# Second MLP: output weights decoded in layer one and kept in DRAM, block sums on VectorE, accumulators read only when complete

## Chip, cores and metric

One core of a Trainium2 chip runs the whole program. The metric is the device time of one execution in microseconds (us); lower is better. Times before the change: 1127.17, 1128.53 and 1132.4 us, median 1128.53 us.

## What is computed

Causal attention with a decay, then two MLPs on its output, all in fp32:

```python
cum = np.cumsum(np.log(np.clip(f, 0.0001, 1.0)), axis=-1)
scores = scale * np.matmul(q, k.transpose(0, 1, 3, 2)) + cum[:, :, :, None] - cum[:, :, None, :]
attn = softmax(where(causal, -1e9, scores))          # q, k, v: 4 x 8 x 576 x 64
x = (attn @ v) -> (2304, 512)
h = x @ w_in;  x = (h - np.tanh(h)) @ w_out          # first MLP, 512 -> 2048 -> 512
h = x @ w_in2; out = np.maximum(h, 0.0) ** 2 @ w_out2  # second MLP, same sizes
```

## The kernel before

Every fp32 operand of a matmul is split into a high and a low part (hi, lo; ScalarE copies the rounded high part, VectorE or GpSimd subtracts it for the low one), and each product is three matmul passes: hi·hi, hi·lo, lo·hi. Attention and the first MLP fill the first 656 us or so; the change leaves their instructions in their order.

The second MLP is computed with seven block products in place of eight (a 2 x 2 block multiplication with sums of blocks ahead of it and additions behind it). It has two layers:

- **Layer one** (`layer1`, 24 units of 7 products: 3 groups of 768 tokens, for each 8 pairs `p` of hidden chunks). A product (`l1_product`, matmul L1072) is 6 matmuls of 384 columns. `after1` reads the PSUM banks: additions on VectorE L1084, a copy L1088 and relu L1098, L1102, L1107 on ScalarE. `store1` squares on GpSimd (L1113) and stores the result `g` to the DRAM scratch `gscr` (L1114).
- **Layer two** (`layer2`, 36 steps `n`: 9 token blocks `j` of 4 steps `q`, 7 products each). A step loads `g` from `gscr` in one DMA (`g_load`, L1154), forms four sums of 256 elements in `g_prep` (GpSimd L1162, L1163, L1165, VectorE L1164) and splits raw blocks and sums (ScalarE L1171, VectorE L1172) into a `gc` tile. A product (`l2_product`, matmul L1191) is 6 matmuls of 256 columns. The seven products share four PSUM banks, two to a bank for 1 and 6, 7 and 2, 5 and 4. After the block's last step `after2` reads them: VectorE L1204, ScalarE copy L1210, one addition on GpSimd L1211; then the output is stored.

The weights arrive in an encoded form: `load_w` fetches a pair, `decode_w` rebuilds the floats (ScalarE L178, L179, VectorE L185, L187), `combine` forms four sums on GpSimd (L229) and splits sums and raw blocks (ScalarE L248, lo parts L249 on GpSimd for the first piece, else VectorE). The output weights (phase 2) take the place of the input weights (phase 1) of the same pair, so they can be decoded only when the last group of tokens has used that pair: one per unit in units 16 to 23, the last ones in layer two.

The order is set in three ways. `cw.later(k, fn)` runs a follow-up after `k` more products; `feed.pace(goal)` starts at most one decode behind each product; and a list scheduler then orders each engine's queue by priority, with a bonus (`L2HOT`) for the start of layer two. SyncE (SP) issues all DMAs from one queue in order; every engine works its queue in order.

Layer two's products, and what their banks wait for:

```python
ORDER2 = (1, 6, 7, 5, 2, 4, 3)
if q == 3:
    cw.later(1, lambda: after2(j, k))       # behind every product
# after2, k == 6: copy bank 0, then
nc.gpsimd.tensor_tensor(t[:, 2], in0=t[:, 0], in1=t[:, 1], op=ALU.add)
# after2, k == 7: reads bank 1, into which product 2 is still to be written
add(t[:, 3], at(7), t[:, 2])
```

## Time and profile before

| | |
|---|---|
| median of 3 runs | 1128.53 us |
| profiled execution: time, span | 1124.71 us, 1123.0 us |
| granted TensorE clock, mean | 0.962 |
| TensorE busy | 1030.2 us (92%) |
| VectorE, ScalarE, GpSimd busy | 767.6, 597.5, 563.6 us |
| layer one of the second MLP | about 661 to 861 us |
| layer two | 861 to 1119 us |

The profile is one execution on the chip. Its page has a line of 40 slices for each engine, with the busy share in tenths; the timeline lists runs of like instructions of one engine with the idle time ahead of them and what ended it; the chain of waits follows the end back to what released each step. A busy TensorE isn't TensorE at its peak: its clock is granted at one of two levels (1.2 and 2.4 GHz), shown as a mean from 0.5 to 1.0. Layer one and layer two are the stages to read, each for itself.

### The profile page before, as it was taken

To read this page: it belongs to the slowest core of one execution; us is meant where nothing else is said; L and a number is where in the kernel's file an instruction comes from. 1 tells how busy PE (TensorE), PEld (TensorE's weight loads), DVE (VectorE), ACT (ScalarE), POOL (GpSimd) and SP (SyncE) were. 2 spreads that over 40 slices of the span, in tenths; PEclk is the share of its full clock that TensorE was granted. 3 is DMA by queue.
4 is the path that set the end of the run, shared out by engine and by line. 5 is a ranking of instruction groups with operands and counts; after the bars stand their busy time and mean duration, and the time that the engine had idled before them with its cause. 6 is when DMAs were issued, how large, how long until landed. Compare 5 with 4: busy or idle time off the path is not lost.

```text
span 1123.0 us, 20534 instructions
## 1 busy us (share of the span) xinstructions
PE 1030.2 (92%) x7246; PEld 981.5 (87%) x7246; DVE 767.6 (68%) x1579; ACT 597.5 (53%) x1256; POOL 563.6 (50%) x709
## 2 busy tenths in 40 slices
PE   7989999999999999999999989999984678888878
PEld 5778899999999999999987778999984678888878
DVE  5889835777777777777557763535688986666662
ACT  6879744666666667666446543434556442332220
POOL 4755523455545554564223444464577864444450
PEclk9999999999999999999999999999987788998899
DMA  8958433432433234321313252344555343332321
GB/s 221 261 171 248 145 96 79 123 84 65 130 86 106 79 93 115 91 69 47 86 59 110 76 160 94 113 144 143 186 171 165 122 132 94 101 107 94 95 94 38
DMA packets 152309, 131.76 MB, mean 117 GB/s; under 512 B 81328, under 2 KB 128752, under 8 KB 152208
## 3 DMA queue, kind: packets, MB, share of 16 engines
q1 hardware_dynamic: 152160, 130.43, 39.4%
q8 instruction: 57, 0.93, 0.3%
q14 instruction: 44, 0.36, 0.1%
q10 hardware_dynamic: 48, 0.03, 0.0%
HBM read 93.13 MB, written 32.58 MB: 112 GB/s over the span
## 4 chain that ended last, share of the span: by engine, by line
PE 54%; DVE 9%; DMA 8%; POOL 8%; issue 6%; ACT 3%; SPq 1%; DVEq 0%; POOLq 0%; ACTq 0%
PE y L915 13%; PE h L875 13%; PE r L1072 10%; DMA graw<-gscr 5%; PE o L1191 5%; DVE gc L1172 4%; PE pt L657 4%; PE pv L728 3%; POOL wsum L229 2%; PE s L619 2%; PE s L620 2%; DMA yr<-yscr 1%; POOL t L1211 1%; DMA wraw<-in_moe_w_in_dram 1%; DVE wfull L187 1%
## 5 line engine op out<-in xcount | busy, mean ns | idle before, releaser
L915 PE MATMUL y<-ghl,w 128*128 128x256 f32 (+1 forms) x1536 | 246.8, 303 | 3.0 <-DVE ghl L896 1.6
L915 PEld LDWEIGHTS y<-ghl,w 128*128 128x128 f32 x1536 | 210.1, 190 | 16.7 <-ACT ghl L892 2.8
L875 PE MATMUL h<-x,w 128*128 128x256 f32 x1344 | 200.0, 290 | 4.8 <-POOL w L201 3.7
L875 PEld LDWEIGHTS h<-x,w 128*128 128x128 f32 x1344 | 174.7, 191 | 9.7 <-POOL w L201 5.0
L1191 PE MATMUL o<-wq,gc 128*128 128x256 f32 x648 | 101.1, 302 | 47.3 <-DVE t L1204 33.2
L1191 PEld LDWEIGHTS o<-wq,gc 128*128 128x128 f32 x648 | 91.7, 208 | 49.7 <-DVE t L1204 35.0
L1191 PE MATMUL o<-ws,gc 128*128 128x256 f32 x864 | 128.1, 302 | 5.7 <-DVE gc L1172 3.3
L1191 PEld LDWEIGHTS o<-ws,gc 128*128 128x128 f32 x864 | 121.4, 212 | 6.4 <-DVE gc L1172 3.7
L450 POOL TENSOR_SCALAR Pb<-neg,ccol 128x384 f32<-128x384 f32 (+2 forms) x96 | 68.7, 715 | 91.7 <-PE pt L657 74.1
L1072 PE MATMUL r<-yt,ws 128*128 128x384 f32 x576 | 110.6, 340 | 2.9 <-DVE ys L925 2.9
L578 POOL TENSOR_SCALAR Pb<-Pb,st 128x384 f32<-128x384 f32 (+2 forms) x96 | 66.7, 695 | 82.2 <-DVE st L574 50.6
L1072 PEld LDWEIGHTS r<-yt,ws 128*128 128x128 f32 x576 | 102.8, 192 | 4.1 <-DVE ys L925 3.6
L1113 POOL TENSOR_TENSOR g<-g 128x768 f32<-128x768 f32 x48 | 75.2, 1582 | 61.6 <-ACT g L1102 59.4
L564 ACT ACTIVATE Pb<-Pb,st 128x384 f32<-128x384 f32 (+2 forms) x96 | 67.6, 704 | 68.0 <-DVE st L555 67.7
L1171 ACT ACTIVATE gc<-graw 128x512 fp32r<-128x512 f32 x72 | 33.7, 515 | 130.0 <-PE o L1191 85.2
L1072 PE MATMUL r<-yt,wq 128*128 128x384 f32 x432 | 88.7, 351 | 14.6 <-ACT g L1098 9.8
L1072 PEld LDWEIGHTS r<-yt,wq 128*128 128x128 f32 x432 | 80.0, 199 | 16.5 <-ACT g L1098 11.1
L555 DVE CUSTOM_DVE_ANT_0 Pb<-s,Pb 64x288 f32<-64x288 f32 (+2 forms) x160 | 73.8, 475 | 14.2 <-PE s L620 7.5
L1162 POOL TENSOR_TENSOR gs<-graw 128x256 f32<-128x256 f32 x36 | 33.6, 934 | 89.8 <-DMA graw<-gscr 86.7
L888 DVE TENSOR_TENSOR g<-h,g 128x512 f32<-128x512 f32 x72 | 49.5, 687 | 39.8 <-ACT g L885 38.4
L229 POOL TENSOR_TENSOR wsum<-wfull 128x256 f32<-128x256 f32 x32 | 31.0, 968 | 81.3 <-DVE wfull L187 80.7
L1172 DVE TENSOR_TENSOR gc<-graw,gc 128x512 fp32r<-128x512 f32 x72 | 63.8, 922 | 8.5 <-ACT gc L1171 8.5
(141 smaller groups left out, 2105.3 us busy)
## 6 DMA issues: line engine op xcount, KB each, us to landing
gscr<-g SPq DMA_DIRECT2D x48, 384.0 KB, 3.1
graw<-gscr SPq DMA_DIRECT2D x36, 512.0 KB, 3.6
wraw<-in_moe_w_in_dram SPq DMA_DIRECT2D x32, 512.0 KB, 4.7
wraw<-in_moe_w_out_dram SPq DMA_DIRECT2D x32, 512.0 KB, 5.2
neg<-cscr SPq DMA_DIRECT2D x32, 288.0 KB, 3.6
qk<-in_k_dram SPq DMA_DIRECT2D x48, 128.0 KB, 2.8
v<-in_v_dram SPq DMA_DIRECT2D x48, 128.0 KB, 2.7
K<-K SPq DMA_DIRECT2D x32, 144.0 KB, 2.4
```

The lines of the kernel that those rows point to most:

```text
L229: nc.gpsimd.tensor_tensor(o, in0=a, in1=b, op=op)
L450: nc.gpsimd.tensor_scalar(pb[:rows, o : o + w], t[:rows, :w], ccol[:rows, ti, b * H + h : b * H + h + 1], 1.0, op0=ALU.add, op1=ALU.mult)
L555: nc.vector.tensor_tensor_reduce(out=d, in0=t[:rows, src : src + m], in1=d, scale=-0.125, scalar=3.0e38 if j == 0 else stat(0, x)[:rows], ...
L564: nc.scalar.activation(d, d, AF.Exp, bias=stat(len(parts) - 1, x)[:rows], scale=-1.0, accum_out=stat(2, x)[:rows])
L578: nc.gpsimd.tensor_scalar(d, d, r, 1.0, op0=ALU.mult, op1=ALU.mult)
L875: nc.tensor.matmul(o, lhsT=win(fc, wh, dc), rhs=xpart(j, dc, xh), start=dc == 0 and wh + xh == 0, stop=dc == ND - 1 and wh == 1)
L888: nc.vector.tensor_tensor(g, t, g, op=ALU.subtract)
L915: nc.tensor.matmul(o, lhsT=wout(fc, wh, i * P, P), rhs=ghl[:, xh, fj * n : fj * n + n], start=s == 0 and fj == 0 and wh + xh == 0 and i % ...
L1072: nc.tensor.matmul(t, lhsT=wprod(1, p, k, wh)[:, dc * P : (dc + 1) * P], rhs=yt[i, k][:, xh, dc], start=k in FIRST and dc == 0 and wh + xh ...
L1113: nc.gpsimd.tensor_tensor(g, in0=g, in1=g, op=ALU.mult)
L1172: nc.vector.tensor_tensor(lo, in0=src, in1=hi.bitcast(F32), op=ALU.subtract)
L1191: nc.tensor.matmul(o, lhsT=gc[n][:, gh, GWHERE[k], e], rhs=wprod(2, 2 * q + e, k, wh), start=q == 0 and e == 0 and gh + wh == 0 and c0 == ...
```

## The change

The weights' two phases part ways. Phase 1 stays as it was, but for new tags, so that raw pieces of four pairs share tiles, and for lo parts, which are now all on VectorE. Phase 2 is decoded and summed during layer one from a raw tile of its own (one decode of phases 1 and 2 at a time), one pair per two units; the four sums and three raw quarters go to a DRAM scratch `wscr` as fp32 in three DMAs (0.92 MB). When the input weights of pair `p` are done with in the last group, `final_load` brings them back in one DMA and `final_split` splits them.

In layer two the four quarters of `g` come in four DMAs of 128 KB straight to their slots, three VectorE instructions form the sums, and hi and lo are one instruction of 1792 elements each. Steps 0 and 1 are loaded and summed in layer one. `gc` has three buffers (before four), the staging tile `graw` two; step n+4 is loaded right behind the split of step n+2. Banks are read only when both their products are done, and GpSimd's addition is on VectorE.

```diff
-L2HOT = 160
+L2HOT = 100
...
     def decode_w(phase, fc):
+        if phase:
+            if busy:
+                pending.append((phase, fc))
+                return
+            busy.append((phase, fc))
...
+        if phase == 2:
+            w = wscr[p]
+            nc.sync.dma_start(w[:, 0:4], sums.rearrange("p (k f) -> p k f", k=4))
+            f4 = full.rearrange("p (k f) -> p k f", k=4)
+            nc.sync.dma_start(w[:, 4:5], f4[:, 0:1])
+            nc.sync.dma_start(w[:, 5:7], f4[:, 2:4])
+            decoded()
+            return
...
-            (nc.gpsimd if x == 0 else nc.vector).tensor_tensor(lo, in0=src, in1=hi.bitcast(F32), op=ALU.subtract)
+            nc.vector.tensor_tensor(lo, in0=src, in1=hi.bitcast(F32), op=ALU.subtract)
...
+    def final_load(p):
+        t = box2["m2"].tile([P, 7, 256], F32, tag="xl", name=f"wst_{p}", bufs=2)
+        stagew[p] = t
+        nc.sync.dma_start(t, wscr[p])
+
+    def final_split(p):
+        t = stagew.pop(p)
+        split_all(2, p, split_plan(2, p, (t[:, 5:7], t[:, 4:5]), [t[:, 0:4]]), 1)
...
     def layer1():
...
-                elif i == 2:
-                    goal = 2 * NF
-            else:
-                goal = 2 * NF
+            if s >= PRE and (s - PRE) % 2 == 0 and (s - PRE) // 2 < NP2:
+                decode_w(2, (s - PRE) // 2)
+            if s >= PRE - 1 and (s - PRE + 1) % 2 == 0 and (s - PRE + 1) // 2 < NP2:
+                load_w(2, (s - PRE + 1) // 2)
+            if s == n - 3:
+                g_load(0)
+                g_load(1)
+            if s == n - 1:
+                g_sums(0)
+            if s == n:
+                g_sums(1)
...
-            if prev is not None and units1[prev][0] == 2:
-                feed.upload(NF + NP2 + units1[prev][1] + 1)
+            for p in range(NP2):
+                if s == last + FREED[p] - 1:
+                    final_load(p)
+                if s == last + FREED[p] + 1:
+                    final_split(p)
+
+    PRE = 5
+    FREED = (1, 2, 3, 3, 5, 6, 7, 7)
...
-    ORDER2 = (1, 6, 7, 5, 2, 4, 3)
+    ORDER2 = (1, 6, 7, 2, 5, 4, 3)
...
+        src = gscr[j // 3][:, j % 3, 4 * q : 4 * q + 4].rearrange("p (e i) (h t) -> p i h e t", i=2, h=2)
+        for slot, h, i in ((0, 1, 0), (5, 0, 0), (7, 1, 1), (6, 0, 1)):
+            nc.sync.dma_start(t[:, slot], src[:, i, h])
+
+    def g_sums(n):
+        t = graws[n]
+        x = t[:, 7]
+        both = bass.AP(tensor=x.tensor, offset=x.offset, ap=[x.ap[0], [0, 2], [1, 2 * P]])
+        nc.vector.tensor_tensor(t[:, 1], in0=t[:, 0], in1=t[:, 5], op=ALU.subtract)
+        nc.vector.tensor_tensor(t[:, 2:4].rearrange("p k e t -> p k (e t)"),
+                                in0=t[:, 0:2].rearrange("p k e t -> p k (e t)"), in1=both, op=ALU.add)
+        nc.vector.tensor_tensor(t[:, 4], in0=t[:, 6], in1=t[:, 3], op=ALU.subtract)
+
+    def g_split(n):
+        t = graws.pop(n)
+        c = box2["m3"].tile([P, 2, 7, 2, P], F32R, tag="gc", name=f"gc_{n}", bufs=3)
         gc[n] = c
...
+        nc.scalar.activation(c[:, 0], t[:, 1:8], AF.Copy)
+        nc.vector.tensor_tensor(c[:, 1], in0=t[:, 1:8], in1=c[:, 0].bitcast(F32), op=ALU.subtract)
...
-        if q == 3:
+        if q == 3 and k in (6, 2, 4, 3):
             cw.later(1, lambda: after2(j, k))
...
-            nc.gpsimd.tensor_tensor(t[:, 2], in0=t[:, 0], in1=t[:, 1], op=ALU.add)
-        elif k == 7:
+            add(t[:, 2], t[:, 0], t[:, 1])
+        elif k == 2:
             t = tmp2[j]
+            add(outs2[j][0][:, :256], at(2), t[:, 0])
             add(t[:, 3], at(7), t[:, 2])
...
         for n in range(NG):
...
             for x, k in enumerate(ORDER2):
                 if x == 1 and n + 2 < NG:
-                    g_prep(n + 2)
+                    g_sums(n + 2)
+                if x == 3 and n + 2 < NG:
+                    g_split(n + 2)
+                    if n + 4 < NG:
+                        g_load(n + 4)
                 cw.step(lambda: l2_product(n, k))
```

In the changed kernel the lines move: matmul of layer one L1138, of layer two L1270, load L1241, sums L1247, L1248, L1250, split L1256 (ScalarE) and L1257 (VectorE), `after2` L1283 and L1289, weight splits L294 and L295, stores to `wscr` L247, L249, L250, load from it L310.

**First excerpt: ScalarE, from the last unit of layer one into layer two.** `wraw`, `wfull`, `wsum`, `ws` and `wq` are weights (raw, decoded, summed, and split), with phase and pair in the name; `g1_23` is `g` of the last unit; `gc` and `graw` belong to steps of layer two. Before:

```order
L1102 ACTIVATE g1_23_10228<-g1_23_10228 128x768
L178 ACTIVATE wfull_2_6_10280<-wraw_2_6_10258 128x512
L179 ACTIVATE wfull_2_6_10280<-wraw_2_6_10258 128x512
L1107 ACTIVATE g0_23_10278<-g0_23_10278 128x3x128
L248 ACTIVATE ws_2_5_10272<-wsum_2_5_10267 128x512
L178 ACTIVATE wraw_2_6_10258<-wraw_2_6_10258 128x512
L179 ACTIVATE wraw_2_6_10258<-wraw_2_6_10258 128x512
L248 ACTIVATE wq_2_6_10324<-wfull_2_6_10280 128x256
L1171 ACTIVATE gc_0_10342<-graw_0_10337 128x512
```

Now:

```order
L294 ACTIVATE wq_2_1_2_10373<-wst_7_10262 128x512
L1171 ACTIVATE g1_23_10305<-g1_23_10305 128x768
L1176 ACTIVATE g0_23_10350<-g0_23_10350 128x3x128
L294 ACTIVATE ws_2_7_10376<-wst_7_10262 128x1024
L294 ACTIVATE wq_2_1_2_10373<-wst_7_10262 128x256
L1256 ACTIVATE gc_0_10393<-graw_0_10112 128x1792
L1256 ACTIVATE gc_1_10396<-graw_1_10117 128x1792
```

The decoding of pair 6 no longer stands around the end of layer one; two splits of pair 7 stand between the last relu and the first split of layer two.

**Second excerpt: VectorE in layer two, around the end of token block 2 (step 11).** `t2_2` and `os_2` belong to the evacuation of block 2, `o1_2` to `o3_2` are its banks. Before:

```order
L1172 TENSOR_TENSOR gc_14_11125<-gs_14_11124,gc_14_11125 128x1024
L1204 TENSOR_TENSOR t2_2_11067<-o1_2_10874,t2_2_11067 128x256
L1204 TENSOR_TENSOR os_2_1_11069<-o2_2_10875,t2_2_11067 128x256
L1204 TENSOR_TENSOR t2_2_11067<-o2_2_10875,t2_2_11067 128x256
L1204 TENSOR_TENSOR os_2_0_11068<-o3_2_10876,t2_2_11067 128x256
L1204 TENSOR_TENSOR os_2_0_11068<-o1_2_10874,t2_2_11067 128x256
L1164 TENSOR_TENSOR gs_16_11236<-graw_16_11228 128x256
L1204 TENSOR_TENSOR os_2_1_11069<-o2_2_10875,t2_2_11067 128x256
```

Now:

```order
L1248 TENSOR_TENSOR graw_13_10948<-graw_13_10948 128x512
L1257 TENSOR_TENSOR gc_12_10998<-graw_12_10895,gc_12_10998 128x1792
L1250 TENSOR_TENSOR graw_13_10948<-graw_13_10948 128x256
L1257 TENSOR_TENSOR gc_13_11056<-graw_13_10948,gc_13_11056 128x1792
L1283 TENSOR_TENSOR t2_2_11045<-t2_2_11045 128x256
L1283 TENSOR_TENSOR os_2_0_11046<-o1_2_10868,t2_2_11045 128x256
L1283 TENSOR_TENSOR t2_2_11045<-o1_2_10868,t2_2_11045 128x256
L1247 TENSOR_TENSOR graw_14_11001<-graw_14_11001 128x256
L1283 TENSOR_TENSOR os_2_1_11047<-o2_2_10869,t2_2_11045 128x256 x2
L1283 TENSOR_TENSOR t2_2_11045<-o2_2_10869,t2_2_11045 128x256
L1248 TENSOR_TENSOR graw_14_11001<-graw_14_11001 128x512
L1283 TENSOR_TENSOR os_2_0_11046<-o3_2_10870,t2_2_11045 128x256
```

Before, step 14 was split ahead of the evacuation; now its sums and its split stand behind it, and the last sum of step 13 behind the split of step 12.

**Third excerpt: SP's queue in layer one.** Stores of `g` have the unit in the name, stores to `wscr` the pair. Before, in units 19 to 21:

```order
L1114 DMA gscr_2_116<-g1_19_9872 384x1x256
L139 DMA wraw_2_3_9991<-in_moe2_w_out_dram 128x1024
L1114 DMA gscr_2_116<-g0_19_9950 384x1x256
L139 DMA wraw_2_4_10080<-in_moe2_w_out_dram 128x1024
L1114 DMA gscr_2_116<-g1_20_9961 384x1x256
```

Now, in units 12 to 14:

```order
L1183 DMA gscr_1_123<-g1_12_9456 384x1x256
L1183 DMA gscr_1_123<-g0_12_9519 384x1x256
L249 DMA wscr_6_93<-wfull_2_6_9796 128x256
L250 DMA wscr_6_93<-wfull_2_6_9796 128x512
L139 DMA wraw_2_7_9877<-in_moe2_w_out_dram 128x1024
L1183 DMA gscr_1_123<-g1_13_9530 384x1x256
L1183 DMA gscr_1_123<-g0_13_9593 384x1x256
L247 DMA wscr_6_93<-wsum_2_6_9865 128x1024
L139 DMA wraw_2_7_9877<-in_moe2_w_out_dram 128x1024
L1183 DMA gscr_1_123<-g1_14_9602 384x1x256
```

The loads of raw output weights moved seven units ahead, and stores to `wscr` stand between the stores of `g`.

## Rows read from the trace of the kernel before

**Rows 1.** The page, 40 slices of the span, busy tenths and granted clock:

```profile
PE   7989999999999999999999989999984678888878
PEclk9999999999999999999999999999987788998899
```

**Rows 2.** Windows: us, then busy us (count) of each engine, PEclk, DMA share, GB/s:

```profile
742.00:744.00 2.00, 2.00 (x14) 2.00 (x13) 1.07 (x3) 0.01 (x1) 1.92 (x2) 1.00 0.98 313
1000.00:1020.00 20.00, 15.77 (x116) 15.57 (x115) 13.56 (x18) 5.38 (x10) 10.30 (x11) 0.85 0.29 93
```

**Rows 3.** Timeline of TensorE, layer one: start, us, instructions, idle before and releaser:

```profile
796.16 2.24 PE L1072 MATMUL r<-yt,wq 128*128 128x384 f32 x12
...
803.44 2.24 PE L1072 MATMUL r<-yt,wq 128*128 128x384 f32 x12
...
813.05 2.35 PE L1072 MATMUL r<-yt,wq 128*128 128x384 f32 x12 [2.16 <-ACT g L1098]
...
824.03 4.21 PE L1072 MATMUL r<-yt,wq 128*128 128x384 f32 x12 [3.42 <-ACT g L1098]
...
845.98 3.47 PE L1072 MATMUL r<-yt,wq 128*128 128x384 f32 x12 [3.42 <-ACT g L1098]
```

**Rows 4.** Timeline of TensorE, layer two: its first, some middle and last instructions:

```profile
873.08 0.80 PE L1191 MATMUL o<-wq,gc 128*128 128x256 f32 x2 [11.86 <-ACT gc L1171]
...
989.50 1.29 PE L1191 MATMUL o<-wq,gc 128*128 128x256 f32 x7 [4.45 <-DVE t L1204]
...
1000.33 0.88 PE L1191 MATMUL o<-wq,gc 128*128 128x256 f32 x6
1001.05 0.88 PE L1191 MATMUL o<-ws,gc 128*128 128x256 f32 x6
...
1118.60 0.52 PE L1191 MATMUL o<-wq,gc 128*128 128x256 f32 x3
```

**Rows 5.** Waits from 840 us on: us in total, times, longest:

```profile
PE o L1191 <- DVE t L1204: 33.2, 9, 4.4
```

**Rows 6.** Chain of waits, end of a token block: start, us, what:

```profile
1013.47 1.67 POOL t L1211
1015.16 0.43 DVE t L1204
1015.64 4.16 PE o L1191 x18
```

**Rows 7.** Groups by form, 656 to 861 us: busy, mean ns, idle before:

```profile
L1113 POOL TENSOR_TENSOR g<-g 128x768 f32<-128x768 f32 x45 | 70.0, 1568 | 61.6 <-ACT g L1102 59.4 <-PE r L1072 1.8 <-POOL g L1113 0.3
L1084 DVE TENSOR_TENSOR g<-r,u 128x384 f32<-128x384 f32 x70 | 37.3, 550 | 43.4 <-DMA gscr<-g 34.1 <-PE r L1072 9.2
...
L187 DVE SCALAR_TENSOR_TENSOR wfull<-wraw 128x512 uint32<-128x512 uint32 x7 | 10.3, 1470 | 0.0
```

**Rows 8.** Line L1021 (loads of 128 KB in runs of 512 B), 700 to 760 us:

```profile
L1021 SPq DMA_DIRECT2D yr<-yscr x12: 378/528/627, 732.1 to 740.4; - x12
...
DMA to landing us min/median/max: 2.6/3.2/4.1
```

**Rows 9.** Groups by form, 861 to 1123 us:

```profile
L1171 ACT ACTIVATE gc<-gs 128x1024 fp32r<-128x1024 f32 x36 | 37.7, 1047 | 14.0 <-POOL gs L1165 8.0 <-DVE gs L1164 5.9
...
L1171 ACT ACTIVATE gc<-graw 128x512 fp32r<-128x512 f32 x36 | 22.7, 629 | 130.0 <-PE o L1191 85.2 <-issue 40.7 <-DMA gscr<-g 2.3
...
L1204 DVE TENSOR_TENSOR os<-o,t 128x256 f32<-128x256 f32 x36 | 14.9, 424 | 9.0 <-PE o L1191 7.3 <-issue 0.3
```

**Rows 10.** Timeline of VectorE and GpSimd, last steps of layer two:

```profile
1092.41 1.74 DVE L1172 TENSOR_TENSOR gc<-gs,gc 128x1024 fp32r<-128x1024 f32 x1
1093.03 1.70 POOL L1211 TENSOR_TENSOR t<-t 128x256 f32<-128x256 f32 x1
...
1098.51 1.03 DVE L1172 TENSOR_TENSOR gc<-graw,gc 128x512 fp32r<-128x512 f32 x2 [0.29 <-ACT gc L1171]
1099.76 1.23 DVE L1172 TENSOR_TENSOR gc<-gs,gc 128x1024 fp32r<-128x1024 f32 x1 [0.22 <-ACT gc L1171]
```

More of the change, by code (lines that the diff above doesn't have):

```diff
@@ L242, in combine @@
-        mixed = [(t1, 2 * x, 2, sums[:, 512 * x : 512 * x + 512].rearrange("p (c f) -> p c f", f=P)) for x in range(2)]
-        work = [(t2, k, n, src) for k, n, src in raw] + mixed
-        def part_split(x):
+        if phase == 2:
[6 more added lines that the diff above has]
+            return
@@ new lines, in combine, with raw_tile @@
+        v = full.rearrange("p (c f) -> p c f", c=ND)
+        s4 = sums.rearrange("p (k f) -> p k f", k=4)
+        work = split_plan(1, p, (v[:, :, 0:P], v[:, 2:4, P : 2 * P]), [s4[:, 0:2], s4[:, 2:4]])
+        split_all(1, p, work, 1)
+    wscr = [dram.tile([P, 7, 256], F32, name=f"wscr_{p}") for p in range(NP2)]
+    SUMTAG = (0, 2, 4, 6, 7, 9, 11, 13)
+    RAWTAG = ((1, 3, 5), (8, 10, 12))
+    rawt = {}
+    def raw_tile(phase, p, x):
+        key = (phase, p // 4, x)
+        if key not in rawt:
+            rawt[key] = wp.tile([P, 2, 4, 256], F32R, tag=f"w{RAWTAG[p // 4][x]}", name=f"wq_{phase}_{p // 4}_{x}", bufs=1)
+        return rawt[key]
@@ new lines, in raw_slots, with split_plan @@
+    def raw_slots(p):
+        r = p % 4
+        single = 3 * r if r == 1 else 3 * r + 2
+        double = 3 * r + 1 if r == 1 else 3 * r
+        return divmod(double, 4), divmod(single, 4)
+    def split_plan(phase, p, raws_, sums_):
+        t1 = wp.tile([P, 2, 4, 256], F32R, tag=f"w{SUMTAG[p]}", name=f"ws_{phase}_{p}", bufs=1)
+        (dx, d0), (sx, s0) = raw_slots(p)
+        td, ts = raw_tile(phase, p, dx), raw_tile(phase, p, sx)
+        wt[phase, p] = [(t1, k) for k in range(4)] + [(td, d0), (td, d0 + 1), (ts, s0)]
+        n = 4 // len(sums_)
+        work = [(t1, n * x, n, src) for x, src in enumerate(sums_)]
+        work += [(td, d0, 2, raws_[0]), (ts, s0, 1, raws_[1])]
+        return work
@@ L246, in part_split, with split_all, one @@
+    def split_all(phase, p, work, lag):
+        def one(x):
             t, k, n, src = work[x]
-            hi, lo = part(t, k, n, 0), part(t, k, n, 1)
+            f = src.shape[-1]
+            hi, lo = (t[:, hl, k : k + n].rearrange("p k f -> p (k f)").rearrange("p (c f) -> p c f", f=f)
+                      for hl in range(2))
             nc.scalar.activation(hi, src, AF.Copy)
-            (nc.gpsimd if x == 0 else nc.vector).tensor_tensor(lo, in0=src, in1=hi.bitcast(F32), op=ALU.subtract)
+            nc.vector.tensor_tensor(lo, in0=src, in1=hi.bitcast(F32), op=ALU.subtract)
@@ L974, in __init__ @@
         def __init__(self):
-            self.items = [(0, fc) for fc in range(NF)] + [(ph, p) for ph in (1, 2) for p in range(NP2)]
+            self.items = [(0, fc) for fc in range(NF)] + [(1, p) for p in range(NP2)]
             self.loaded = self.decoded = 0
@@ L1052, in stage_load @@
     def stage_load(i):
-        t = box2["m2"].tile([P, 5, 2, NU1], F32, tag="xl", name=f"yr_{i}", bufs=1)
-        r = dict(zip((3, 7, 1, 2, 5), (t[:, x] for x in range(5))))
+        r = {}
+        for ks in ((3, 7), (1, 2)):
+            t = box2["m2"].tile([P, 2, 2, NU1], F32, tag="xl", name=f"yr_{i}_{ks[0]}", bufs=2)
+            r.update(zip(ks, (t[:, 0], t[:, 1])))
+        r[5] = spare()[:, 3 * NU1 : 5 * NU1].rearrange("p (c n) -> p c n", c=2)
         for k in (6, 4):
@@ L1057, in stage_load, with spare @@
         y_load(i, r)
+    spares = []
+    def spare():
+        if not spares:
+            spares.append(wp.tile([P, 5 * NU1], F32, tag="w14", name="spare", bufs=1))
+        return spares[0]
     def blocks3(x):
@@ L1117, in layer1 @@
         n = len(units1)
+        last = n - NP2
         for s in range(n + 1):
@@ L1239, in layer2 @@
         with tc.high_priority(offset=L2HOT):
-            for n in range(2):
+            g_split(0)
+        with tc.high_priority(offset=L2HOT // 2):
+            g_split(1)
+            for n in (2, 3):
                 g_load(n)
-            for n in range(2):
-                g_prep(n)
-                for _ in range(4):
-                    cw.step()
         for n in range(NG):
-            if n + 2 < NG:
-                g_load(n + 2)
-            if n < 4:
-                feed.upto(NF + NP2 + min(NP2, 2 * n + 2))
             for x, k in enumerate(ORDER2):
                 if x == 1 and n + 2 < NG:
-                    g_prep(n + 2)
+                    g_sums(n + 2)
[3 more added lines that the diff above has]
+                        g_load(n + 4)
                 cw.step(lambda: l2_product(n, k))
-                feed.pace(NF + 2 * NP2)
     x_tile(0)
```

96 lines of the change are left out of this document (38 added, 58 removed).

## The prediction

> **What bounds the kernel now.** I read the page first. TensorE is busy nearly everywhere up to slice 29; from slice 30 (814 us) on its digits fall and the granted clock falls with them [rows 1]. The change touches only what lies there, the last 460 us, so I read the two layers of the second MLP each for itself; attention and the first MLP keep their order and their time.
>
> *Layer one* runs without a gap in its middle: the same group of matmuls starts at 796.16 and at 803.44, a unit of 7 products in 7.28 us, 1.04 us each. Then it starts at 813.05, 824.03 and 845.98, the last three units apart from the first: 10.98 us a unit [rows 3]. TensorE waits for ScalarE (relu L1098), whose queue there also holds the decoding of the output weights, one pair a unit, and the clock falls with the waits: 12 matmuls that took 2.24 us take 4.21 after a wait of 3.42, though only 2.35 after a wait of 2.16 [rows 3].
>
> *Layer two* starts 11.86 us after layer one's last matmul (873.08 less 11.86: 861.2) and ends at 1119.1 [rows 4]: 257.9 us. Six matmuls take 0.72 us (from 1000.33 to 1001.05), so 36 steps of 42 matmuls are 5.04 us each, 181.4 us in all; 76 us are waits and low clock. A middle stretch shows nothing full: TensorE 15.77 of 20 us, VectorE 13.56, GpSimd 10.30, the DMA engines 0.29, clock 0.85 [rows 2]. One wait repeats once per token block, 33.2 us over 9 [rows 5], 4.45 in one case [rows 4]. The chain shows what it is: GpSimd's addition takes 1.67 us, VectorE's reading of bank 1 0.43, and only then TensorE may write product 2 into that bank [rows 6].
>
> **The change part by part.**
>
> *The tail of layer one.* At 7.28 us a unit the group of 813.05 would start at 810.72, and that of 845.98 at 832.56: 13.4 us earlier. From 845.98 nine products are left, 9.36 us, so the layer would end at 841.9 and not at 861.2: **-19.3**. The first excerpt shows why it should: the decoding has left ScalarE's queue there.
>
> *What layer one gets for it.* Eight decodes, now in two units (14.56 us) each. VectorE has ten additions of 0.55 in them [rows 7], and a decode's four instructions and four lo parts, which I bound by 1.47 each from the dearest of them [rows 7], 11.8: 17.3 at worst, over the 14.56; at 0.66 each, as I work out below for 512 elements unhindered, 10.8. GpSimd has four squares of 1.57 [rows 7] and four sums, at most 1.67 each like its other addition of 256 elements [rows 6]: 13.0. ScalarE, at 0.63 for 512 elements [rows 9], has eight more, 5.0. It fits, tightly in units 7 and 15, where the tokens of the next group are split too. Price: nothing, up to one lost period of the tail per decode, 8 x 3.70 = 30. The tail had a decode in every unit, the change in every second, so I take the near end: **+4**, one such loss.
>
> *DMA in layer one.* Per two units 1.57 MB of `g`, 1.05 of raw weights, 0.92 to `wscr` and later back. In the fullest stretch 0.63 MB took 2 us at a share of 0.98 [rows 2], 3.1 us per MB: 11.1 of 14.56 us. Hidden, with little to spare. On SP each is an issue of about half a microsecond [rows 8], nine in 14.56 us; but a store to `wscr` waits for GpSimd's sums with the next store of `g` and the next raw load queued behind it (third excerpt).
>
> *The start of layer two.* Behind the last product stand an addition (0.55), two short activations (at most 0.63 each), a split of 1024 on ScalarE (1.05) [rows 7, 9], and then step 0's split. For 1792 elements I extend the rows: ScalarE 0.629 for 512 and 1.047 for 1024 [rows 9], 0.82 per 1000 elements, so 1.67; VectorE 1.03 for 512 and 256 together and 1.23 for 1024 [rows 10], 1.12 per 1000 and 0.09 fixed, so 2.09, and 0.66 for 512. Sum **6.6** before steady work, in place of 11.86 and stalls.
>
> *VectorE's speed.* That took the durations with GpSimd idle. Beside GpSimd's addition at 1093.03 the split of 1024 took 1.74 us, with GpSimd idle 1.23 [rows 10]; the changed kernel has no GpSimd work in layer two. Per step VectorE then has sums 0.42 + 0.66 + 0.42, a split of 2.09 and a quarter of seven additions of 0.42 [rows 9], 4.3 of 5.04 us. At 1.74/1.23 of that it would be 6.1, above TensorE. The Trainium skill ("GPSIMD Engine Reference", Specifications) says that GpSimd shares its SBUF interface with VectorE, with contention for instructions with two SBUF inputs; the rows agree, and by it the 4.3 stands.
>
> *The bank wait* goes: nothing is read before its bank is complete (ORDER2, `after2`). What is late next is the data. Two staging tiles pass load, sums and split, and VectorE takes things in its order (second excerpt). I walk one token block from the end of the split of step 10, in us: load of 12, three more issues of 0.53 and 3.2 to landing [rows 8], 4.8; last sum 0.42; ScalarE 1.67; VectorE 2.09; last sum of 13 0.42; 1.67; 2.09; evacuation 7 x 0.42 = 2.9; sums of 14 1.5; 1.67; 2.09, the split of 14. That is 21.3, and with nine hand-overs of 0.05 (from 1015.59 to 1015.64 in [rows 6]) 21.8, where TensorE needs 20.16. So the loop paces, by 1.6 us a block: 8 x 1.6 = **13**. Bounds: landing at 2.6 and 4.1 [rows 8] moves it by -0.6 and +0.9 a block, and more where a second landing comes on the path; every instruction 5% off moves it by 0.8. So 0 to about 27.
>
> *Clock.* The first wait, of 6.6, costs 2.0 like the one of 3.42; eight waits of 1.6, like the one of 2.16, 0.1 each: **3**.
>
> *At nothing:* tags, the order of additions, and the evacuation at the very end, which is as long as before.
>
> **Sum.** Layer two 6.6 + 181.4 + 13 + 3 = 204.0 against 257.9: -53.9. Span 1123.0 - 19.3 + 4 - 53.9 = 1053.8; with the 1.7 that lie around the span (1124.71) 1055.5. The median of the runs shown is 3.8 above the profiled execution; I add half, as three runs spread over 5: **1057**.
>
> **A rule against the change.** Twelve loads of 128 KB were issued within 8.3 us and each landed 2.6 to 4.1 us after its issue [rows 8]; one after the other they would need 38, so they overlap. The Trainium skill ("DMA: Bandwidth & Descriptors", Bandwidth and Anatomy of one DMA) wants DMAs of 1 MiB and more, and gives about 2.0 us plus bytes/436e3 for one: as an estimate 2.3 us for 128 KB, 9.2 for four in turn where the loop has 4.8, 35 us more over 8 blocks, 1092. By that rule the third rival would be the likeliest; the rows show loads side by side and leave it the chance it has.
>
> **The rivals.**
> - *TensorE paces layer two.* If loads land at 2.6 and sums hide beside other work, the loop is below 20.16 and the 13 go: 1057 - 13 - 1 = 1043. For it: the second and third landing need not be on the path. Against: VectorE's in-order queue. Chance 0.18.
> - *Layer one stalls again.* A square, a sum or a relu behind a decode, or SP held by a `wscr` store: from 4 to 8 lost periods of 3.70 less the 4 counted, 11 to 26 more: 1068 to 1083. For it: VectorE's worst case is over its time. Against: units 796 to 810 run unbroken with squares and stores. Chance 0.13.
> - *The loop is longer.* Four loads at once land later (4.1 or more, both landings on the path), 2 to 4 us more a block: 1073 to 1089; at the far end they are served in turn, 4 x 2.6 = 10.4 in place of 4.8, 45 us more: 1102. For it: 512 B runs in fours. Against: DMA share 0.29 now. Chance 0.12.
> - *VectorE stays slow* without GpSimd: 6.1 a step, 36 x 1.06 = 38 more than TensorE's pace, 1057 - 13 + 38 = 1082, and more with the loop. The rows of the last steps speak against it: 0.03.
> - *Slower than before:* the 14.7 MB through `wscr` make layer one bound by transfers. To reach 1128 plus half a percent it must lose 77 us in eight pairs of units, 9.6 us each: 3.54 MB in 24 us, below 150 GB/s. Rows show 313 GB/s at share 0.98 [rows 2]. 0.02.
> - *The change doesn't do what it says* (decoding still in the tail): the excerpts show it gone. Nil.
>
> **How the numbers follow.** The forecast has 0.52, from 1048 to 1066. The range 1039 to 1080 takes in nearly all of the first rival and over half of layer one's and some of the third: 0.52 + 0.16 + 0.09 + 0.05 = 0.82. A measurement here tells about 0.5% (6 us) from no change; every case but the one slower is 40 us or more below 1128.5, and some of that chance I leave to cases not thought of: faster 0.95, same 0.02, slower 0.03.
>
> **What would show it.** Layer one ends near 846 with units of 7.28 us up to the end. The first steady matmul of layer two comes 6 to 7 us later. TensorE's waits for VectorE's reading of banks are gone; in their place a wait of about 1.6 us at the third step of each block, for the split. VectorE's split of 1792 takes about 2.1 us, pieces of `graw` land in about 3.2. GpSimd is idle in layer two. Units of 11 us in layer one, splits of 3 us, or landings above 5 would make it wrong.

## The result and the profile after

The changed kernel takes 1075.65 us (median of 4 runs, 1074.40 to 1076.56) against 1127.85 us (4 runs) before: ratio 0.953, 95% interval 0.950 to 0.957. The profiled execution took 1074.4 us with a span of 1072.7. That is faster, as forecast, and inside the range, but 18.7 us above the 1057. Two errors of opposite sign lie behind this: layer one ended 27.1 us later than forecast (873.0, not 845.9), and layer two took 8.3 us less (195.7, not 204.0; before 257.9). That the time is inside the range is in part luck: layer one's miss by itself makes 1084, outside it.

The page, against [rows 1]: from slice 34 on, in layer two, TensorE's digits are 9 up to the last and GpSimd is idle. What is left stands in slices 27 to 33, from 697 to 885 us, where GpSimd works too.

```profile
PE   7989999999999999999999999988788869999997
...
POOL 4763622465455654556411333655655440000000
```

The windows say the same, against [rows 2]: 100 us of layer one with TensorE busy for 82.62, 160 us of layer two with 159.78.

```profile
750.00:850.00 100.00, 82.62 (x442) 77.21 (x442) 62.69 (x94) 44.19 (x77) 55.05 (x42) 0.98 0.65 213
```

```profile
890.00:1050.00 160.00, 159.78 (x1332) 159.58 (x1331) 122.53 (x171) 55.77 (x39) 0.00 (x0) 1.00 0.43 126
```

TensorE's timeline, against [rows 3, 4]. The waits of [rows 3] have moved forward: three of the longer ones now lie at 726, 756 and 774. Groups of 12 that take 2.24 us at full clock take 3.25 and 3.51. Layer one ends at 881.43 less 8.39, 873.04. Layer two has one wait of note behind its start, at 1058.70, and ends at 1068.8.

```profile
726.36 3.25 PE L1138 MATMUL r<-yt,wq 128*128 128x384 f32 x12 [2.40 <-ACT g L1167]
...
755.73 1.31 PE L1138 MATMUL r<-yt,ws 128*128 128x384 f32 x6 [2.27 <-DVE g L1150]
...
774.49 3.51 PE L1138 MATMUL r<-yt,wq 128*128 128x384 f32 x12 [2.86 <-ACT g L1167]
...
881.43 0.80 PE L1270 MATMUL o<-wq,gc 128*128 128x256 f32 x2 [8.39 <-ACT gc L1256]
...
1058.70 0.74 PE L1270 MATMUL o<-wq,gc 128*128 128x256 f32 x4 [1.89 <-DVE gc L1257]
...
1067.91 0.88 PE L1270 MATMUL o<-wq,gc 128*128 128x256 f32 x6
```

The waits from 661 to 873 us name the cause's neighbours. TensorE waits for VectorE's additions and for ScalarE's relu (24.1 us in all), VectorE's decode (L200) waits 21.8 us for ScalarE's, and ScalarE itself waits 28.4 us, in eight waits, for raw weights to land:

```profile
DVE wfull L200 <- ACT wfull L194: 21.8, 5, 6.3
ACT wfull L193 <- DMA wraw<-in_moe_w_out_dram: 21.4, 5, 5.5
...
PE r L1138 <- DVE g L1150: 15.1, 14, 2.4
...
PE r L1138 <- ACT g L1167: 9.0, 5, 2.9
ACT wraw L193 <- DMA wraw<-in_moe_w_out_dram: 7.0, 3, 4.3
```

The chain of waits shows how the two hang together. VectorE ends a decode (L202), GpSimd forms its sums (L244), SP may then store them (L247), and only behind that store can it issue the next raw load (L139). The load lands 5.51 us later. The next decode already stands in ScalarE's queue, ahead of the relu (L1167); the relu waits with it, and TensorE for the relu:

```profile
716.62 0.80 POOL wsum L244 x2
...
718.79 0.33 SPq L247
...
719.69 5.51 DMA wraw<-in_moe_w_out_dram
...
725.27 0.06 ACT wfull L193
...
725.83 0.48 ACT g L1167
...
726.36 3.26 PE r L1138 x12
```

Layer two, VectorE behind the end of a token block: seven additions of the evacuation with the sums of the next step between them, then a pair of splits.

```profile
966.13 0.42 DVE L1283 TENSOR_TENSOR t<-t 128x256 f32<-128x256 f32 x1
966.47 0.42 DVE L1283 TENSOR_TENSOR os<-o,t 128x256 f32<-128x256 f32 x1
...
969.39 0.42 DVE L1250 TENSOR_TENSOR graw<-graw 128x256 f32<-128x256 f32 x1
...
971.71 3.96 DVE L1257 TENSOR_TENSOR gc<-graw,gc 128x1792 fp32r<-128x1792 f32 x2 [0.37 <-ACT gc L1256]
```

The groups from 873 us on give the durations that the forecast extended, 1.70 us on ScalarE (forecast 1.67) and 2.02 on VectorE (2.09):

```profile
L1257 DVE TENSOR_TENSOR gc<-graw,gc 128x1792 fp32r<-128x1792 f32 x36 | 72.1, 2024 | 21.6 <-ACT gc L1256 21.4
L1256 ACT ACTIVATE gc<-graw 128x1792 fp32r<-128x1792 f32 x36 | 60.5, 1699 | 117.4 <-DVE graw L1250 107.1 <-PE o L1270 7.5 <-DVE wq L295 2.8
```

and the loads of `g` (line L1241) their landing, against [rows 8]:

```profile
DMA to landing us min/median/max: 2.1/2.6/4.1
```

### The profile page after: what moved, and what is told of

It reads as the page before. It is cut to its first block, busy times and chain, and to the rows that moved or that the text cites. A ratio compares the mean times of both kernels' runs of the same rounds, so it can differ in the third digit from the quotient of the medians.

```text
span 1072.7 us, 20563 instructions
## 1 busy us (share of the span) xinstructions
PE 1014.9 (95%) x7246; PEld 963.7 (90%) x7246; DVE 755.3 (70%) x1596; ACT 587.0 (55%) x1176; POOL 435.5 (41%) x576
## 5 line engine op out<-in xcount | busy, mean ns | idle before, releaser
L1256 ACT ACTIVATE gc<-graw 128x1792 fp32r<-128x1792 f32 x36 | 60.5, 1699 | 117.4 <-DVE graw L1250 107.1
L1138 PE MATMUL r<-yt,ws 128*128 128x384 f32 x576 | 111.0, 340 | 12.9 <-DVE g L1150 12.8
L1138 PEld LDWEIGHTS r<-yt,ws 128*128 128x128 f32 x576 | 100.9, 190 | 18.2 <-DVE g L1150 13.6
L1270 PE MATMUL o<-ws,gc 128*128 128x256 f32 x864 | 117.0, 285 | 0.0
L1270 PEld LDWEIGHTS o<-ws,gc 128*128 128x128 f32 x864 | 110.4, 194 | 0.0
L1182 POOL TENSOR_TENSOR g<-g 128x768 f32<-128x768 f32 x48 | 80.3, 1683 | 54.2 <-ACT g L1171 36.3
L1270 PE MATMUL o<-wq,gc 128*128 128x256 f32 x648 | 92.3, 287 | 10.5 <-ACT gc L1256 8.4
L1138 PE MATMUL r<-yt,wq 128*128 128x384 f32 x432 | 86.6, 343 | 11.9 <-ACT g L1167 9.0
L1270 PEld LDWEIGHTS o<-wq,gc 128*128 128x128 f32 x648 | 84.7, 195 | 11.5 <-ACT gc L1256 8.7
L1138 PEld LDWEIGHTS r<-yt,wq 128*128 128x128 f32 x432 | 76.8, 192 | 15.2 <-ACT g L1167 10.6
L1257 DVE TENSOR_TENSOR gc<-graw,gc 128x1792 fp32r<-128x1792 f32 x36 | 72.1, 2024 | 21.6 <-ACT gc L1256 21.4
L720 DVE TENSOR_TENSOR PT<-pt,PT 128x384 fp32r<-128x384 f32 (+2 forms) x96 | 55.1, 574 | 10.3 <-ACT PT L719 5.6
L951 DVE TENSOR_TENSOR ghl<-g,ghl 128x512 fp32r<-128x512 f32 x72 | 53.8, 747 | 10.2 <-ACT ghl L947 9.9
```

The lines of the kernel that those rows point to most:

```text
L720: cw.later(LAG['trlo'], lambda: nc.vector.tensor_tensor(dst[1], src, dst[0].bitcast(F32), op=ALU.subtract))
L1138: nc.tensor.matmul(t, lhsT=wprod(1, p, k, wh)[:, dc * P : (dc + 1) * P], rhs=yt[i, k][:, xh, dc], start=k in FIRST and dc == 0 and wh + xh ...
L1182: nc.gpsimd.tensor_tensor(g, in0=g, in1=g, op=ALU.mult)
L1256: nc.scalar.activation(c[:, 0], t[:, 1:8], AF.Copy)
L1257: nc.vector.tensor_tensor(c[:, 1], in0=t[:, 1:8], in1=c[:, 0].bitcast(F32), op=ALU.subtract)
L1270: nc.tensor.matmul(o, lhsT=gc[n][:, gh, GWHERE[k], e], rhs=wprod(2, 2 * q + e, k, wh), start=q == 0 and e == 0 and gh + wh == 0 and c0 == ...
```

## The experiments

In the profiles of these kernels E is the end of layer one, the first steady matmul of layer two less the wait ahead of it. In the changed kernel it is 873.0. Ratios and their 95% intervals are to the kernel before, run again beside each group of experiments; its median was 1130.6 us beside 1 to 4, 1131.8 beside 5 to 8, 1134.4 beside 9 to 11 and 1131.0 beside 12, against 1127.85 beside the change. So a time in us compares with the change's to some 3 to 7 us only, and the traces (one of each kernel) say where it went.

**1. No decoding in layer one**: what the new work costs there in all.

```diff
-        nc.sync.dma_start(t, wscr[p])
+        nc.sync.dma_start(t.rearrange("p k f -> p (k f)"), gscr[0].rearrange("p b c n -> p (b c n)")[:, 0:1792])
...
-            if s >= PRE and (s - PRE) % 2 == 0 and (s - PRE) // 2 < NP2:
-                decode_w(2, (s - PRE) // 2)
-            if s >= PRE - 1 and (s - PRE + 1) % 2 == 0 and (s - PRE + 1) // 2 < NP2:
-                load_w(2, (s - PRE + 1) // 2)
```

> The changed kernel without the decoding of the output weights: no raw loads, no decode, no sums and no stores to the scratch; the final load takes as many bytes from the scratch of g instead, so layer two multiplies other numbers, at the same instructions. Theory (what layer one lost, from 842 us where it would have ended to 873, is the decoding): layer one ends at 842 to 848 us, TensorE waits less than 6 us in it, time 1047 us (1043 to 1053). Rival A (the loss has other causes: lo parts now on VectorE, the token splits in units 7 and 15): layer one still ends after 860, time 1063 or more.

Measured: 1040.8 us (ratio 0.921, 0.915 to 0.927), E 838.1, and layer two as long as with the decoding (195.6 us). That is the theory, and a little below its numbers; TensorE waits 1.0 us in the layer. So the decoding costs layer one 35 us, and the tail's gain was there in full: 838.1, where the forecast had 841.9 ahead of this price.

**2. The next raw load ahead of the sums' store.** It is issued when the last read of the raw tile has been queued.

```diff
+                if phase == 2 and fc + 1 < NP2:
+                    load_w(2, fc + 1)
...
-            if s >= PRE - 1 and (s - PRE + 1) % 2 == 0 and (s - PRE + 1) // 2 < NP2:
-                load_w(2, (s - PRE + 1) // 2)
+            if s == PRE - 1:
+                load_w(2, 0)
```

> The changed kernel with one edit: the load of the next raw weights is given right behind the last read of the raw tile, so that in the DMA queue it stands ahead of the store of the four sums, not behind it. Theory (a loop through in-order queues: the raw load waits in SP's queue for GpSimd's sums, ScalarE waits in order for its landing, VectorE and GpSimd behind ScalarE): ScalarE's waits for raw weights, 28 us in the changed kernel, fall below 15, and half of the loss comes back: 1058 to 1066 us. Rival B (VectorE and GpSimd have too much to do in these units, whatever the order): within 3 us of 1075.6.

Measured: 1070.7 us (0.946, 0.941 to 0.952), E 869.5. Neither theory's number came. The waits for raw weights are down from 28.4 to 2.8 us, but others took their place. `wfull` and the sums share a ring of two tiles, and the next decode now waits until the sums' store has left the tile:

```profile
ACT wfull L193 <- DMA wscr<-wsum: 20.8, 6, 5.6
```

**3. The first ScalarE instruction of a decode kept in program order**, so that the scheduler can't put it ahead of the relu.

```diff
-            nc.scalar.activation(lo_, words[:, :, 0], AF.Copy, scale=0.936 * 2.0 ** -29)
+            ins = nc.scalar.activation(lo_, words[:, :, 0], AF.Copy, scale=0.936 * 2.0 ** -29)
+            if phase == 2 and x == 0:
+                tc.keep_in_program_order(ins)
```

> The changed kernel with one edit: the first ScalarE instruction of each decode of output weights is kept in program order on its engine, so that it stands one to two units later than where the scheduler had pulled it. Theory (ScalarE stands in order ahead of its data): its waits for raw weights fall below 8 us, layer one ends before 860, time 1052 to 1064 us. Rival B (too much work whatever the order): within 3 us of 1075.6.

Measured: 1073.4 us (0.950, 0.946 to 0.954), E 866.8. By the time this is rival B, and no difference to the change that is clear of noise. But it was half an experiment: the decode's second instruction (L196 here) was still put ahead, and waits in the first one's place.

```profile
ACT wfull L196 <- DMA wraw<-in_moe_w_out_dram: 15.9, 5, 5.3
```

The start of layer two grew from 8.39 to 12.10 us as well.

**4. Experiments 2 and 3 together.**

```diff
...
+            if phase == 2 and x == 0:
+                tc.keep_in_program_order(ins)
...
+                if phase == 2 and fc + 1 < NP2:
+                    load_w(2, fc + 1)
...
```

> Both edits, the raw load ahead and the decode kept in program order. Theory: waits for raw weights nearly gone, layer one ends at 846 to 854 us, time 1048 to 1058 us. Rival B (too much work whatever the order): 1070 us or more.

Measured: 1072.3 us (0.949, 0.945 to 0.952), E 867.6: by the time rival B again. The ring's wait stays, and one wait of TensorE is new: the decode of the last input weights stands behind the first one of output weights, now held at its place, waits for the ring there, and its split (L298) comes late.

```profile
720.73 1.01 PE L1142 MATMUL r<-yt,ws 128*128 128x384 f32 x2 [6.29 <-ACT ws L298]
```

**5. The early load, and sums in tiles of their own** (two of 512 elements, from another ring).

```diff
-        sums = wide(f"wsum_{phase}_{p}", F32)
...
+            halves = [m1.tile([P, 512], F32, tag="g", name=f"wsum_{p}_{x}", bufs=3) for x in range(2)]
...
-            nc.sync.dma_start(w[:, 0:4], sums.rearrange("p (k f) -> p k f", k=4))
+            for x in range(2):
+                nc.sync.dma_start(w[:, 2 * x : 2 * x + 2], halves[x].rearrange("p (k f) -> p k f", k=2))
```

> The raw load ahead (as before in this study) and one edit more: the four sums of output weights get tiles of their own, two of 512 elements that layer one leaves unused, so that the two decode buffers hold decoded weights alone; the store of the sums becomes two DMAs. Theory C (after the raw load was put ahead, ScalarE waited 20.8 us for the store of the sums to land, because the next decode needs that buffer: the loop closes over the two buffers): those waits fall below 6 us, layer one ends before 860, time 1055 to 1064 us. Rival B (VectorE and GpSimd have too much to do in these units): within 4 us of 1070.7.

Measured: 1066.7 us (0.944, 0.940 to 0.947), E 864.9: 4 less than experiment 2, at the edge of rival B's range and short of the theory's. The ring's waits are gone. With nothing else to hold them, the decodes were put earlier in ScalarE's queue again, and wait for the raw data once more:

```profile
ACT wfull L193 <- DMA wraw<-in_moe_w_out_dram: 17.0, 6, 5.5
```

**6. The transfers alone**: loads and stores as in the change, from a tile of zeros, and no instruction of the decoding.

```diff
+        if phase == 2:
+            wraw.pop((phase, fc))
...
+            for x in range(2):
+                nc.sync.dma_start(w[:, 2 * x : 2 * x + 2], z)
+            nc.sync.dma_start(w[:, 4:5], z[:, 0:1])
+            nc.sync.dma_start(w[:, 5:7], z)
+            decoded()
+            return
```

> The changed kernel with the loads of raw output weights and the stores to the scratch (from a tile of zeros, in four DMAs), but without decode and sums; layer two multiplies by zeros. Rival D (the transfers themselves, 14.7 MB more, slow the stores of g and with them layer one): time 1055 or more, layer one ends after 852. Theory B or C (the work on the engines and its order, not the transfers): within 5 us of the run without any decoding, 1036 to 1046 us.

Measured: 1046.5 us (0.925, 0.921 to 0.929), E 841.7, 3.6 over experiment 1. The transfers and SP's issues for them are not the cost, as long as no store among them waits for a result.

**7. The decoding without GpSimd's sums.**

```diff
-        sums = wide(f"wsum_{phase}_{p}", F32)
+        sums = wide(f"wsum_{phase}_{p}", F32) if phase == 1 else full
...
-        for o, a, b, op in ops:
+        for o, a, b, op in (ops if phase == 1 else ()):
...
-            nc.sync.dma_start(w[:, 0:4], sums.rearrange("p (k f) -> p k f", k=4))
+            nc.sync.dma_start(w[:, 0:4], full.rearrange("p (k f) -> p k f", k=4))
```

> The changed kernel with the output weights decoded, but without the four sums on GpSimd; the decoded weights are stored in their place, so layer two's numbers are others. Theory E (GpSimd's four sums per decode are what costs: squares stand behind them in order, and VectorE's instructions run slow beside them): most of the 35 us comes back, 1042 to 1056 us. Rival F (the cost lies with ScalarE and VectorE, whose decode instructions stand ahead of relu and additions): 1062 or more.

Measured: 1064.0 us (0.941, 0.936 to 0.946), E 862.8: rival F. Without the sums ScalarE still waits 27.3 us for raw weights (28.4 in the changed kernel).

So the sums are 10.2 of the 35 us, and the decode on ScalarE and VectorE, with its waits for raw weights, 21.1 (862.8 less 841.7). The two runs lie 5.1 us apart and the trace is of the longer one, so the sums' part may be larger.

**8. The kernel before with the new evacuation alone**: the order of the products, banks read when complete, GpSimd's addition on VectorE.

```diff
-    ORDER2 = (1, 6, 7, 5, 2, 4, 3)
+    ORDER2 = (1, 6, 7, 2, 5, 4, 3)
...
-        if q == 3:
+        if q == 3 and k in (6, 2, 4, 3):
...
-            nc.gpsimd.tensor_tensor(t[:, 2], in0=t[:, 0], in1=t[:, 1], op=ALU.add)
+            add(t[:, 2], t[:, 0], t[:, 1])
...
```

> The kernel before with one part of the change alone: the order of products in a token block and the reading of banks only when complete, with GpSimd's addition on VectorE. Theory (the bank wait, 33.2 us over 9 blocks, set layer two's end; data would have come in time): 30 to 42 us faster, 1086 to 1099 us. Rival (GpSimd's sums and the loads set the pace by themselves, so that TensorE waits for data in place of banks): less than 15 us faster, 1113 or more.

Measured: 1100.6 us (0.973, 0.970 to 0.976); layer two takes 227.7 us, 30 less than before. That is the theory's gain at its near end (31 us less than the kernel before beside it), but its reason holds in part only. The bank waits of [rows 5] are gone; the data doesn't come in time, and TensorE now waits for splits 20 times in 36 steps, 21.7 us in all. From 974 to 1043 us every step has such a wait, and they lie 6.3 us apart in the mean where 42 matmuls need 5.04:

```profile
992.65 1.45 PE L1191 MATMUL o<-ws,gc 128*128 128x256 f32 x10 [0.91 <-DVE gc L1172]
...
998.72 1.45 PE L1191 MATMUL o<-ws,gc 128*128 128x256 f32 x10 [0.78 <-DVE gc L1172]
```

Behind them, in its waits, is the way of the data over GpSimd's sums. The bank waits had hidden it. (These are idle times of GpSimd and ScalarE, not of TensorE.)

```profile
POOL gs L1162 <- DMA graw<-gscr: 78.2, 27, 4.1
ACT gc L1171 <- POOL gs L1165: 65.1, 30, 4.8
```

**9. Both orders at once**: experiment 5 with both first ScalarE instructions of a decode (from pair 1 on) and the first of each final split kept in program order.

```diff
+            if phase == 2 and fc and x == 0:
+                tc.keep_in_program_order(ins[0])
...
+                tc.keep_in_program_order(ins[1])
...
+            if phase == 2 and x == 0:
+                tc.keep_in_program_order(ins)
```

> Raw load ahead and sums in tiles of their own, and now both ScalarE instructions that open a decode (from the second pair on) and the first of each final split are kept in program order; in the two earlier runs of that kind only the first of the two was, and the second was still pulled ahead of its data. Theory C (in-order queues: whatever stands on ScalarE ahead of its data holds relu, VectorE and GpSimd behind it): ScalarE's waits for raw weights and for stores to the scratch fall below 4 us, layer one ends at 846 to 856 us, time 1050 to 1060 us, faster than the changed kernel by 15 or more. Rival B (VectorE, slowed by GpSimd beside it, has too much to do): within 4 us of 1066.7.

Measured: 1064.0 us (0.940, 0.935 to 0.944): by the time rival B. But E is 857.1, 7.8 less than in experiment 5, and the waits for raw weights are down to 2.3 us. The final splits, held too, came late, and layer two's start gave back 4.6 us of it (13.21 for 8.57):

```profile
870.29 0.79 PE L1283 MATMUL o<-wq,gc 128*128 128x256 f32 x2 [13.21 <-ACT gc L1269]
```

**10. The change with the bank reading of before**: old order, a reading behind each product, the addition on GpSimd.

```diff
-    ORDER2 = (1, 6, 7, 2, 5, 4, 3)
+    ORDER2 = (1, 6, 7, 5, 2, 4, 3)
...
-        if q == 3 and k in (6, 2, 4, 3):
+        if q == 3:
...
-            add(t[:, 2], t[:, 0], t[:, 1])
+            nc.gpsimd.tensor_tensor(t[:, 2], in0=t[:, 0], in1=t[:, 1], op=ALU.add)
...
```

> The changed kernel with the order of products, the reading of banks and GpSimd's addition as they were before. Theory (the bank wait is a wait of its own, once a block, and TensorE has little else to wait for in layer two): TensorE waits 3 to 4.4 us in each of 9 blocks again, 27 to 42 us slower with the clock, 1102 to 1118 us. Rival (the load and split loop is nearly as long as TensorE's block and runs on in the meantime, so that only the part of the wait beyond its slack counts): less than 20 us slower, below 1096.

Measured: 1088.4 us (0.961, 0.955 to 0.966), the rival's range: 12.7 more than the change, 8 by the ratios. Layer two takes 211.2 us, 15.5 more. A bank wait is at most 2.7 us, where it was 4.4 in [rows 5], although GpSimd's addition takes 1.94 us here; GpSimd has no sums of blocks left, and the addition starts right behind ScalarE's copy:

```profile
PE o L1270 <- DVE t L1283: 12.5, 9, 2.7
```

**11. The change with two of the three sums of a step on GpSimd.**

```diff
-        nc.vector.tensor_tensor(t[:, 1], in0=t[:, 0], in1=t[:, 5], op=ALU.subtract)
+        (nc.vector if n < 2 else nc.gpsimd).tensor_tensor(t[:, 1], in0=t[:, 0], in1=t[:, 5], op=ALU.subtract)
...
-        nc.vector.tensor_tensor(t[:, 4], in0=t[:, 6], in1=t[:, 3], op=ALU.subtract)
+        (nc.vector if n < 2 else nc.gpsimd).tensor_tensor(t[:, 4], in0=t[:, 6], in1=t[:, 3], op=ALU.subtract)
```

> The changed kernel with two of the three block sums of each step, from step 2 on, on GpSimd as before. Theory (VectorE's instructions run 1.2 to 1.4 times as long beside GpSimd's, and the loop gets longer): the split of 1792 takes 2.2 us or more on the mean, TensorE waits for splits in every block, 10 to 35 us slower, 1086 to 1111. Rival (GpSimd takes work off VectorE, whose queue is the loop): within 5 us of 1075.6 or faster.

Measured: 1088.5 us (0.960, 0.955 to 0.966), 12.8 more than the change, 8 by the ratios; the profiled execution was the shortest of four (1082.35), and its layer two is 10.7 us longer (206.4). The theory's time came, near its lower end, and not its mechanism: the splits on VectorE slowed little, 2.07 us for 2.02. A sum takes 1.14 us in the mean on GpSimd and 0.42 on VectorE, so the loop got longer by its sums, and TensorE waits for it twelve times:

```profile
L1257 DVE TENSOR_TENSOR gc<-graw,gc 128x1792 fp32r<-128x1792 f32 x36 | 74.3, 2070 | 58.6 <-ACT gc L1256 58.6
...
L1247 POOL TENSOR_TENSOR graw<-graw 128x256 f32<-128x256 f32 x34 | 38.6, 1135 | 60.2 <-DMA graw<-gscr 60.0
```

```profile
PE o L1270 <- DVE gc L1257: 11.1, 12, 2.3
```

**12. Experiment 9 without holding the final splits.** Against experiment 9:

```diff
-            ins = nc.scalar.activation(hi, src, AF.Copy)
-            if phase == 2 and x == 0:
-                tc.keep_in_program_order(ins)
+            nc.scalar.activation(hi, src, AF.Copy)
```

> As the run with the decode kept behind its data (raw load ahead, sums in their own tiles, both opening ScalarE instructions of a decode in program order), but the final splits left to the scheduler again. In that run layer one ended at 857 us, but its last units took 8.8 to 9.2 us and layer two began 13.2 us later; with the final splits not held, the last units took 7.3 us and the gap was 8.6. Theory: both add up, layer one ends at 849 to 855 us, layer two begins 7.5 to 9.5 us later, time 1051 to 1058 us, faster than both kernels. Rival: decodes that end later push the final splits into the last units whatever their order, and the time stays above 1061.

Measured: 1058.4 us (6 runs, 1055.89 to 1061.81; 0.936, 0.933 to 0.939), just above what the theory had, and the best version: 1.6% below the change (1058.4 against 1075.65), 6.4% below the kernel before. E is 854.3, as the theory had it, the start of layer two 9.99. What is left of TensorE's waits in layer one is spread out, 12.3 us in 11 waits, most for VectorE's additions and the relu. The start:

```profile
864.30 0.79 PE L1281 MATMUL o<-wq,gc 128*128 128x256 f32 x2 [9.99 <-ACT gc L1267]
```

## Why the prediction was right or wrong

**The tail of layer one, -19.3: right.** Experiment 1 ends the layer at 838.1, where the term gives 841.9. Once the decoding is away, the units at the end run unbroken.

**What layer one gets for it, +4: wrong, and this is the step that failed.** It measured +31 (873.0 less 841.9), the far end of the bound (8 x 3.70 = 30). The step added up each engine's busy time per two units, found that it fits, and took one lost period. In the profile the engines still have room: over the 100 us of the windows VectorE works 62.69 and GpSimd 55.05. What doesn't fit is the order. The prediction saw the pieces, a `wscr` store waiting for GpSimd with the next raw load behind it, and named them as its second rival, which is what happened (27.1 us more, where it had 11 to 26); it gave it 0.13. It had no row for a decode ahead of its own data in ScalarE's queue, with the relu behind it. The tail's loss, one period per decode, was the nearest row, and I argued it away by the doubled spacing.

The runs split the 35 us that experiment 1 measures: 3.6 transfers, 21.1 the decode on ScalarE and VectorE with its waits, 10.2 the sums (differences of single profiles of kernels whose runs spread by 1 to 5 us). Of the same 35, 18.7 come back by order and tiles alone, with all the work still done (873.0 to 854.3, experiment 12). Each half measure moved the wait one place on: from the raw load to the ring (2), from the first instruction to the second (3), from the ring back to the raw load (5). By the times alone the experiments' rival B (too much work for VectorE and GpSimd, whatever the order) fits experiments 3, 4, 5 and 9; it is experiment 12 and the ends of layer one that speak for the order, and for those 18.7 us only. What the 12.6 us between 854.3 and 841.7 are stays open; VectorE's longer instructions beside GpSimd (below) are a candidate, and no run separates them.

**DMA hidden: right.** 3.6 us by experiment 6, SP's issues included.

**The start of layer two, 6.6: 8.39.** The sum had the final split of pair 7 by its part on ScalarE (1.05) and left out the lo parts on VectorE, 3.1 us in the chain, behind which step 0's split begins. On the other side it counted VectorE's part of step 0's split (2.09), and TensorE starts without it. The size was off by 1.8, and experiments 9 and 12 show that what is queued there moves it (13.2, 10.0). The chain of the changed kernel:

```profile
876.58 1.47 DVE ws L295
878.04 1.62 DVE wq L295
...
879.68 1.71 ACT gc L1256
```

**36 steps of 5.04: right**, and **VectorE unhindered: right**, 2.02 us a split.

**The loop, +13: too large; the first rival (0.18) was nearer in number.** One wait of 1.89 us, and one of 0.22 ahead of it, is all there is. Three blocks of the loop, from 971.71 to 1033.72, take 20.7 us each in the mean (20.5 to 21.0), against 21.8 walked and 20.16 for TensorE. So the loop is the longer one, as forecast, by 0.5 us a block and not by 1.6, and for that long TensorE doesn't wait: the splits still have a lead. The wait comes with the next block, which takes 22.9 (to 1056.62). In its chain SP needs 1.83 us for one issue, where the median is 0.47; why is open.

```profile
1033.72 3.96 DVE L1257 TENSOR_TENSOR gc<-graw,gc 128x1792 fp32r<-128x1792 f32 x2 [0.37 <-ACT gc L1256]
...
1056.62 4.00 DVE L1257 TENSOR_TENSOR gc<-graw,gc 128x1792 fp32r<-128x1792 f32 x2
```

```profile
1036.72 1.83 SPq L1241
```

The walk was right in its path. Its sizes were not: landing 2.6 and not 3.2 (the lower bound), 2.02 and not 2.09 for two splits, and evacuation with sums 3.7 us (966.13 to 969.81) and not 4.4, since VectorE starts its small instructions 0.33 us apart though each lasts 0.42. Those are 1.4 us together.

**Clock, 3: about 4.** Layer two's 195.7 less 8.39, 181.4 and 1.89 leaves 4.0, most of it at the low clock behind the start: the first 60 matmuls take 10.35 us (881.43 to 891.78) where full clock needs 7.2.

**The bank wait: right that it goes, but its worth is not its sum of waits.** Of the 62 us that layer two lost, the bank part alone brings 30 (experiment 8), and everything but it 47 (257.9 to the 211.2 of experiment 10). The two overlap by 15, and either cure alone uncovers the other's limit. The prediction read only the end of the chain [rows 6], the addition and the reading of bank 1. Further back in the same chain of the kernel before stand a load and three sums of a later step, with the addition (from 1013.47 on) behind them in GpSimd's queue, 3.3 us after ScalarE's copy was done (1010.14). The addition stands right behind such sums in seven of the nine blocks; much of the "bank wait" was thus a wait for data and sums, and in experiment 10, with no sums there, it is 1.4 us in the mean:

```profile
1006.52 3.84 DMA graw<-gscr
...
1010.50 0.99 POOL gs L1162
...
1011.55 1.06 POOL gs L1163
...
1012.68 0.78 POOL gs L1165
```

**The rule against the change** (the Trainium skill, "DMA: Bandwidth & Descriptors", Bandwidth and Anatomy of one DMA, weighed in the prediction) is not borne out for these loads. That four go in turn was the prediction's reading, and the page's figure is for DMAs that GpSimd issues; SyncE issues these. Four of 128 KB, issued some 0.47 us apart, land 2.6 us after their issue each (medians), so the last some 4 us after the first issue, and not 9.

## What to carry to other kernels

Work moved beside a busy stage is not priced by adding busy times: follow what it is queued behind, and what is queued behind it, on every in-order queue, SP's included. If an instruction can stand ahead of its data in such a queue, price it as one stall per occurrence until a run shows otherwise, and cure load order, buffers and place in the queue together, since here one alone mostly moved the wait. Follow a wait back to its beginning: the engine that ends it may have stood behind other work in its own queue. Of two limits that hide each other, price the pair, not each.
